# Two attentions on one core: score 0 ahead of the split maximum, and two kinds of copies moved between ScalarE and VectorE

## The chip, the core and the metric

The kernel runs on one core of one Trainium2 chip. The core has a matrix engine (TensorE, PE in the profile, with its weight loads listed apart as PEld), VectorE (DVE), ScalarE (ACT), GpSimd (POOL), and SyncE (SP), which issues most DMAs. Each engine works off its own queue in order; they meet through semaphores. Matmul results land in PSUM, which has eight banks of 128 × 512 f32; this kernel uses seven as a pool (bank0 to bank6) and keeps the eighth (`po`) for the value products. The metric is device time in microseconds, one launch; smaller is better.

## What is computed

Two independent multi-head attentions over 2048 positions, 576 features and 32 heads of 18, with their outputs side by side. Cut to what matters:

```python
# A: each position attends to itself and 7 earlier ones, 2 apart
idx = pos[:, None] - 2 * jnp.arange(8)[None, :]
logits = einsum("bhsd,bhswd->bhsw", q, kg) * scale       # masked where idx < 0
o_a = einsum("bhsw,bhswd->bhsd", softmax(logits), vg)
# B: full attention, 2048 x 2048 per head
p = softmax(einsum("bhqd,bhkd->bhqk", q, k) * scale)
o_b = einsum("bhqk,bhkd->bhqd", p, v)
out = concatenate([o_a @ wo_a, o_b @ wo_b], axis=-1)     # q, k, v = x @ wqkv for each
```

## The kernel before

**Stages.** First come the projections of both parts (L353, L290), mixed with the first maxima. Then a loop over 512 steps does the full attention of part B. Part A's windowed attention runs beside it on GpSimd, with little pieces on the other engines. The output products of both parts are slipped in between.

**The loop over steps.** The heads stand in eight groups `g` of four, the queries in four blocks `b` of 512, the keys in sixteen tiles `kt` of 128; a step is one `(g, b, kt)`, and a block is 16 steps. For each of the four heads of a step, `score` (L256) lets TensorE multiply 128 keys by 512 queries into a bank of the ring "scores" (banks 0 to 3), and ScalarE takes the exponential into a tile `e` (L268). `weigh` (L728), one step later, multiplies `e` by the values into `po` (L731), which adds up over the block's 16 key tiles. The values carry a column of ones, so `po` holds the denominators too.

**Maxima.** The exponential needs each query's maximum over all keys subtracted. The kernel finds it a good way ahead: the scores are computed a second time, transposed, with queries on the partitions (L160), and VectorE reduces a bank to maxima (L168). Once a block has all of them, they are negated, transposed, split and loaded by small DMAs into the spare rows 54 and 55 of the query tile `qs` (`place`, L191), so that the score matmul of 56 rows subtracts them itself. These banks come from the ring "else" (banks 4 to 6). All in all 2048 pieces of 512 keys are reduced.

**Rows of the array.** A head's 54 rows (18 features, three times, as split numbers) lie in the partitions 0 to 63 or 64 to 127, so two matmuls of different halves run at once. Score order in a step is h = 0, 2, 1, 3: 0 and 2 lie in the lower rows, 1 and 3 in the upper.

**Split maxima.** A step gives VectorE three reductions: two of whole pieces (`maximum`, L218, one from each half) and one of a bank that is filled by two half pieces of 256 keys (`parts_of_maximum`, L233), the first from the upper rows and the second from the lower. [...] So the second half waits for a no-op in ScalarE's queue (L243), and that no-op waits for the first half. The no-op is issued before the step's first exponential.

**Order in a step** (L1140 to L1180), as TensorE's queue has it: first half, score 0, whole maximum (upper), score 2, score 1, second half, [an output product, if one is due, "inside" the step], score 3, whole maximum (lower), then the value products of the step before. VectorE gets the reductions in the order whole, split, whole.

**Output products.** A product of part A (`sums_of_a`, L946) or B (`sum_of`, L1044) multiplies by `wo` in two row halves into two banks, `one` and `two` (`beside`, L1022). For A ScalarE copies one sum and VectorE adds the other. For B VectorE copies `one` (L1055) and adds `two` (L1056). Those of B run "inside" a step with `kind` "scores" while more than four pieces of maxima are left, and otherwise stand in `waiting` with no kind; `waiting` is worked off after the scores of a step or at its end. When the maxima have run out, two steps share one run of value products (`paired`), which here is called the tail.

**End of a block.** `finish` (L736) copies `po` into the tile `o` with ScalarE (L740, 31 times; the last block goes through `closing`). A DMA, a reciprocal and GpSimd's multiplication then divide by the denominators, many steps later (L763 to L770). The first value product of the next block waits for this copy, since it overwrites `po`. `producing` is the set of steps in which, by the plan, an output product stands: part A's at `A_FROM + GAP * j + ends[h] + 1` (L973), and B's near the end (L1128). `total` is the number of maxima pieces, `given` counts those already issued.

## Time and profile before

| | |
|---|---|
| Median of 3 runs | 1619.34 us (1617.29 to 1619.95) |
| The profiled execution: its own time | 1616.82 us |
| Its span, first to last instruction | 1615.0 us |
| Mean granted TensorE clock | 0.997 |
| Busy in the stretch 560 to 580 us (of 20.00) | PE 20.00, VectorE 18.68, ScalarE 20.00, GpSimd 19.21 |
| Busy in the stretch 1560 to 1600 us (of 40.00) | PE 40.00, VectorE 10.32, ScalarE 21.63, GpSimd 0.00 |

The page is of one execution; times in it are in us from the span's start. Matmuls overlap at their ends, and so do the instructions of ScalarE and VectorE, so a pace is read from start to start. A bracket at the end of a timeline row gives the idle time before it and what ended that, inferred from semaphores. PE and its weight loads are listed as two engines: PEld can be idle while PE is busy.

### The profile page before, as it was taken

How to read it: one execution, taken by the hardware profiler on the slowest of the kernel's cores; microseconds unless marked ns; L12 is line 12 of the kernel's file. 1: busy time of each engine (PE TensorE's matmuls, PEld its weight loads, DVE VectorE, ACT ScalarE, POOL GpSimd, SP SyncE). 2: the span in 40 equal slices, each digit the busy share in tenths (PEclk: the TensorE clock that was granted, in tenths of full speed). 3: DMA queues.
4: the chain of work that ended last, by engine and by line, in shares of the span. 5: the costliest groups of instructions: out<-in, count | busy, mean ns of one | idle time of the engine just before them, and what ended most of it. 6: DMA issues, size and time to landing. Idle time of an engine off the chain costs nothing.

```text
span 1615.0 us, 35230 instructions
## 1 busy us (share of the span) xinstructions
PE 1599.0 (99%) x13394; PEld 959.5 (59%) x13394; DVE 1393.9 (86%) x2366; ACT 1212.4 (75%) x2419; POOL 961.1 (60%) x792
## 2 busy tenths in 40 slices
PE   9999999999999999999999999999999999999998
PEld 7999888999544444444444444444444444445676
DVE  5199999999899998999999999999999999999532
ACT  6424442121799998999999999999999999998444
POOL 2405742210265995996995995995996997920000
PEclk9999999999999999999999999999999999999999
DMA  8937954432222262254235235332532241034201
GB/s 250 239 121 196 275 164 133 134 104 79 60 56 64 73 147 54 62 118 113 62 85 133 72 98 115 98 91 60 125 106 58 59 135 47 22 124 139 89 38 60
DMA packets 186058, 172.11 MB, mean 107 GB/s; under 512 B 119152, under 2 KB 132976, under 8 KB 184160
## 3 DMA queue, kind: packets, MB, share of 16 engines
q1 hardware_dynamic: 181024, 158.31, 35.3%
q0 software_dynamic: 4032, 10.63, 3.1%
q8 instruction: 105, 1.72, 0.5%
q10 hardware_dynamic: 832, 0.92, 0.2%
q14 instruction: 65, 0.53, 0.1%
HBM read 96.94 MB, written 71.90 MB: 105 GB/s over the span
## 4 chain that ended last, share of the span: by engine, by line
PE 82%; POOL 7%; DVE 5%; DMA 3%; ACT 2%; issue 1%; SPq 0%; POOLq 0%; DVEq 0%; ACTq 0%
PE po L731 24%; PE bank L160 15%; PE bank L353 15%; PE bank L263 15%; PE bank L1036 8%; PE bank L290 5%; DVE mx L168 4%; ACT e L268 2%; POOL pr L868 1%; POOL pr L872 1%; POOL pr L911 1%; DMA akv<-da 1%; DMA dqk<-olo 1%; POOL pr L912 1%; POOL pr L913 0%
## 5 line engine op out<-in xcount | busy, mean ns | idle before, releaser
L168 DVE TENSOR_REDUCE mx<-bank 128x2 f32<-128x512 f32 x2048 | 1286.0, 684 | 114.5 <-PE bank L160 86.2
L268 ACT ACTIVATE e<-bank 128x512 f32<-128x512 f32 x2048 | 1050.2, 607 | 90.3 <-PE bank L263 83.2
L160 PE MATMUL bank<-ks,qs 54*128 54x256 f32 (+1 forms) x2536 | 791.8, 377 | 7.4 <-DVE mx L168 5.9
L160 PEld LDWEIGHTS bank<-ks,qs 54*128 54x128 f32 x2536 | 411.3, 184 | 464.6 <-DVE mx L168 423.4
L263 PE MATMUL bank<-qs,ks 56*128 56x512 f32 x2048 | 567.3, 426 | 0.1
L731 PE MATMUL po<-e,v 128*19 128x512 f32 x4096 | 537.9, 599 | 0.0
L263 PEld LDWEIGHTS bank<-qs,ks 56*128 56x128 f32 x2048 | 299.3, 185 | 14.7 <-issue 7.5
L868 POOL TENSOR_TENSOR pr<-aq,akv 128x1024 f32<-128x1024 f32 x72 | 158.5, 2202 | 15.4 <-DMA akv<-da 12.8
L911 POOL TENSOR_TENSOR pr<-lg,akv 128x1024 f32<-128x1024 f32 x72 | 158.5, 2201 | 0.6
L872 POOL TENSOR_TENSOR pr<-pr 128x1024 f32<-128x1024 f32 x64 | 152.6, 2384 | 5.0
L731 PEld LDWEIGHTS po<-e,v 128*19 128x19 f32 x4096 | 70.5, 97 | 129.4 <-issue 127.0
L681 ACT ACTIVATE ohi<-bank 128x512 f32<-128x512 f32 (+1 forms) x56 | 30.4, 595 | 152.5 <-issue 100.7
L353 PE MATMUL bank<-xhi,ahi 64*128 64x512 f32 (+1 forms) x448 | 113.5, 387 | 0.0
L353 PE MATMUL bank<-xhi,alo 64*128 64x512 f32 (+1 forms) x448 | 112.3, 387 | 0.0
L353 PE MATMUL bank<-xlo,ahi 64*128 64x512 f32 (+1 forms) x448 | 111.9, 388 | 0.1
L912 POOL TENSOR_TENSOR pr<-pr 128x512 f32<-128x512 f32 x72 | 92.5, 1285 | 5.6
L401 POOL TENSOR_TENSOR alo<-raw,ahi 128x512 fp32r<-128x512 f32 (+1 forms) x14 | 17.6, 1258 | 120.7 <-ACT ahi L400 88.8
L493 POOL TENSOR_TENSOR olo<-olo,ohi 128x512 fp32r<-128x512 f32 x36 | 46.2, 1294 | 66.1 <-ACT ohi L492 57.5
L767 POOL TENSOR_TENSOR o<-o,rec 128x512 f32<-128x512 f32 x29 | 37.6, 1297 | 58.7 <-ACT e L268 34.2
L103 POOL CAST mh<-mt 128x32 fp32r<-128x32 f32 x32 | 6.9, 217 | 102.3 <-DVE mt L183 99.5
L353 PEld LDWEIGHTS bank<-xhi,ahi 64*128 64x128 f32 (+1 forms) x448 | 65.0, 181 | 2.9
L353 PEld LDWEIGHTS bank<-xhi,alo 64*128 64x128 f32 (+1 forms) x448 | 63.9, 182 | 2.9
(197 smaller groups left out, 1827.6 us busy)
## 6 DMA issues: line engine op xcount, KB each, us to landing
do<-n SPq DMA_DIRECT2D x28, 512.0 KB
da<-ohi SPq DMA_DIRECT2D x52, 256.0 KB
akv<-da SPq DMA_DIRECT2D x64, 175.5 KB
out<-y SPq DMA_DIRECT2D x32, 288.0 KB
qs<-dqk SPq DMA_DIRECT2D x30, 288.0 KB
ks<-dqk SPq DMA_DIRECT2D x30, 288.0 KB
at<-dao SPq DMA_DIRECT2D x64, 128.0 KB
rec<-drec SPq DMA_DIRECT2D x29, 256.0 KB
```

Of the source, the lines that this page charges most:

```text
L160: return nc.tensor.matmul(ps if part is None else ps[:, 256 * r : 256 * r + 256], qs[at, b, p, 128 * t : 128 * t + 128], ks[at, p, 512 * k ...
L168: nc.vector.tensor_reduce(at, ps.rearrange("q (s n) -> q s n", s=2), axis=AX.X, op=ALU.max)
L263: nc.tensor.matmul(ps, ks[at, p, 128 * kt : 128 * kt + 128], qs[at, b, p], start=True, stop=True)
L268: nc.scalar.activation(e, ps, AF.Exp, scale=SCALE)
L290: nc.tensor.matmul(ps, a, b, start=c == i == 0, stop=c == 4 and i == 1)
L353: nc.tensor.matmul(ps, a, b, start=start, stop=stop)
L731: nc.tensor.matmul(po[32 * i : 32 * i + 19], vs[g][:, kt, 19 * i : 19 * i + 19], es[i], start=kt == 0, stop=kt == NT - 1)
L868: nc.gpsimd.tensor_mul(pr, ap(st["q"][:, 2 * c], (SUB, 2), (0, W), (1, SUB)), window(st["k"], c))
L872: nc.gpsimd.tensor_add(st["pr"], st["pr"], pr)
L911: nc.gpsimd.tensor_mul(at, ap(st["lg"], (0, 2), (SUB, W), (1, SUB)), window(st["v"], c))
L912: nc.gpsimd.tensor_add(at[:, :, :4], at[:, :, :4], at[:, :, 4:])
L1036: nc.tensor.matmul(ps, a, b, start=start, stop=stop)
```

## The change

Four edits, printed with their core:

```diff
-    def score(g, b, kt, h, kind="scores"):
+    def score(g, b, kt, h, kind="scores", between=None):
...
         nc.tensor.matmul(ps, ks[at, p, 128 * kt : 128 * kt + 128], qs[at, b, p], start=True, stop=True)
+        if between:
+            between()
...
-        nc.scalar.activation(o, po, AF.Copy)
+        if step + 1 in producing or sum(given) == total:
+            nc.scalar.activation(o, po, AF.Copy)
+        else:
+
+            nc.vector.tensor_copy(o, po)
+            copied.add(step + 1)
...
     producing = set()
+    copied = set()
...
         one, two = beside(kind, *both)
-        nc.vector.tensor_copy(y, one)
+        if kind:
+            nc.vector.tensor_copy(y, one)
+        else:
+            nc.scalar.activation(y, one, AF.Copy)
         nc.vector.tensor_add(y, two, y)
...
-        parts = bool(begun) or total - sum(given) > 3
+        parts = (bool(begun) or total - sum(given) > 3) and step not in copied
 
         ps = bank() if inside and whole else None
-        if parts:
-            part = parts_of_maximum()
+        part = []
         for h in (0, 2, 1, 3):
 
             if inside and h == 3:
                 inside.pop(0)()
-            es[h] = score(g, b, kt, h)
+
+            es[h] = score(g, b, kt, h, between=(lambda: part.append(parts_of_maximum())) if parts and h == 0 else None)
             if h == 0 and whole:
                 maximum(1, ps)()
             if h == 1 and parts:
-                part()
+                part[0]()
```

In each step with a split maximum, score 0's matmul is issued to TensorE ahead of the first half; the no-op on ScalarE still stands ahead of the first exponential. At the end of a block, where no output product is planned for the next step and maxima are left, VectorE copies `po` in ScalarE's place, and the next step goes without its split maximum, whose two halves are made later. In products of B without a kind, ScalarE copies `one`, and VectorE still adds `two`.

In the built programs, six of the 31 block copies go to VectorE, and 27 of the 30 copies of half a product's sums to ScalarE. The six steps without a split maximum move twelve half pieces on; at the end of the maxima two products of B, which stood in `waiting`, now run inside steps. The number of reductions, 2048, and all other instructions stay.

## The prediction

> **What bounds the kernel now.** I read the page's busy line first, then its chain of waits, then two stretches of the busy-time windows. The columns of a window row are its bounds and length, then the busy time (and count of instructions) of TensorE, its weight loads, VectorE, ScalarE and GpSimd, then granted clock, DMA share and GB/s.

> ```profile
> PE 1599.0 (99%) x13394; PEld 959.5 (59%) x13394; DVE 1393.9 (86%) x2366; ACT 1212.4 (75%) x2419; POOL 961.1 (60%) x792
> PE 82%; POOL 7%; DVE 5%; DMA 3%; ACT 2%; issue 1%; SPq 0%; POOLq 0%; DVEq 0%; ACTq 0%
> ...
> 560.00:580.00 20.00, 20.00 (x160) 8.55 (x154) 18.68 (x32) 20.00 (x40) 19.21 (x18) 1.00 0.50 119
> 1560.00:1600.00 40.00, 40.00 (x470) 29.63 (x466) 10.32 (x23) 21.63 (x43) 0.00 (x0) 1.00 0.10 38
> ```

> In the long stage (the row at 560) TensorE and ScalarE never rest and VectorE hardly does; in the tail (the row at 1560) only TensorE is full. So the question is what sets the pace of one step of the long stage. The timeline of one step answers it; its columns are start, length, engine, line and operation, and the count.

> ```profile
> 558.80 0.38 PE L160 MATMUL bank<-ks,qs 54*128 54x256 f32 x1
> 558.81 0.49 PE L263 MATMUL bank<-qs,ks 56*128 56x512 f32 x1
> 559.03 0.40 PE L160 MATMUL bank<-ks,qs 54*128 54x512 f32 x1
> 559.14 0.52 PE L263 MATMUL bank<-qs,ks 56*128 56x512 f32 x2
> 559.38 0.30 PE L160 MATMUL bank<-ks,qs 54*128 54x256 f32 x1
> 559.51 0.44 PE L263 MATMUL bank<-qs,ks 56*128 56x512 f32 x1
> 559.51 0.43 PE L160 MATMUL bank<-ks,qs 54*128 54x512 f32 x1
> 559.87 1.05 PE L731 MATMUL po<-e,v 128*19 128x512 f32 x8
> 560.86 0.38 PE L160 MATMUL bank<-ks,qs 54*128 54x256 f32 x1
> ...
> 558.80 0.18 PEld L160 LDWEIGHTS bank<-ks,qs 54*128 54x128 f32 x1 [0.85 <-DVE mx L168]
> ...
> 559.29 0.18 PEld L160 LDWEIGHTS bank<-ks,qs 54*128 54x128 f32 x1
> ...
> 561.34 0.18 PEld L160 LDWEIGHTS bank<-ks,qs 54*128 54x128 f32 x1
> 561.43 0.29 PE L160 MATMUL bank<-ks,qs 54*128 54x256 f32 x1
> ...
> 561.56 0.40 PE L160 MATMUL bank<-ks,qs 54*128 54x512 f32 x1
> 561.89 0.14 PEld L731 LDWEIGHTS po<-e,v 128*19 128x19 f32 x8 [0.25 <-issue]
> ...
> 581.21 0.38 PE L160 MATMUL bank<-ks,qs 54*128 54x256 f32 x1
> ...
> 1556.45 1.91 PE L731 MATMUL po<-e,v 128*19 128x512 f32 x16
> 1558.30 0.73 PE L263 MATMUL bank<-qs,ks 56*128 56x512 f32 x4
> ```

> From 558.80 to 581.21 lie 11 steps, so a plain step takes 2.037 us. The "0.85 <-DVE mx" before its first weight load looks like a wait for VectorE, but TensorE is busy with the value products (L731) in that time: the next matmul follows them 0.99 us after they begin (559.87 to 560.86). In the tail, where nothing of VectorE is awaited, sixteen of them take 1.85 us (1556.45 to 1558.30), so eight cost 0.86 and the rest, 0.99, is what eight alone take before anything can follow. The pace is therefore TensorE's own: about 1.05 us from the first half maximum to the first value product, then 0.99.

> What fills the 1.05 us is the handshake of the split maximum. The second half (559.38, rows 0 to 63) may not start before the first half (558.80) is done, and ScalarE's no-op carries that message. The first half ends at 559.18, and the second half's weight load starts 0.11 us later, at 559.29; one step on, 561.24 and 561.34. After it come the second half, the whole maximum 0.13 later, the products 0.33 to 0.36 later. Nothing waits there but for that message.

> **The change, part by part.**

> *Score first.* Score 0 and the first half run on different halves of the array and start within 0.01 us of each other, so swapping them alone moves nothing. But the no-op does not wait for one matmul. In the built program every matmul that signals raises one counter of TensorE, in order, and the no-op waits for a value of it. Before, that value is reached with the first half; in the new order score 0 is counted ahead of it, so the no-op waits for both. The rows above give the two ends: the half of 256 columns ends at 559.18, the score of 512 at 559.30. The message thus leaves 0.12 us later, less the 0.01 by which score 0 starts earlier: 0.11.

> [...]

> How much of 0.11 reaches the step? Take the faster step, from 560.86: weight load at +0.48, second half +0.57, whole maximum +0.70, products +1.03, next step +1.03+0.99 = 2.02. Adding 0.11 to each gives 2.13, against the mean of 2.037: 0.09. The slower step (558.80: load +0.49, second half +0.58, whole maximum +0.71, products +1.07) has 0.04 of other delay in it, which hides behind the new one. Lower bound: zero, if the second half's place were set by its row group, which ends score 2 about then. Upper bound: 0.115 with ScalarE's first exponential, queued behind the no-op, later too. I take 0.08, near the upper end, because the load follows the message in both steps at the same distance.

> How many steps pay is in the rows grouped by line (count, then busy time and mean ns; the first row is count, then shortest, median and longest ns).

> ```profile
> L243 ACTq EVENT_SEMAPHORE  x488: 17/17/17, 418.8 to 1504.8; - x163
> ...
> L168 DVE TENSOR_REDUCE mx<-bank 128x2 f32<-128x512 f32 x2048 | 1286.0, 684 | 114.5 <-PE bank L160 86.2 <-PE bank L353 0.5
> ...
> L740 ACT ACTIVATE o<-po 128x512 f32<-128x512 f32 x31 | 19.5, 628 | 2.5 <-issue 2.5
> ...
> L954 ACT ACTIVATE y<-bank 128x288 f32<-128x288 f32 x32 | 13.2, 412 | 18.2 <-PE bank L1036 17.4 <-issue 0.9
> ...
> L1055 DVE COPY y<-bank 128x288 f32<-128x288 f32 x24 | 10.9, 456 | 49.0 <-PE bank L1036 49.0
> ```

> Of 488 handshakes 32 stand in steps with a product of part A and 62 in the two steps beside each of the 31 copies: 394 plain steps at 0.08 are 31.5 us. The 32 product steps are full on TensorE as well, at 0.10: 3.2. In the 62 the exponentials, late by the copy, cover most of it: I take 0.03, 1.9 (none to 0.11 are the bounds). Cost so far 36.6 us.

> The score first also gains. At the first step of a block, score 0 waits for its block's negated maxima from many DMA queues; before, these waits are worked off only after the first half is issued.

> ```profile
> 482.73 0.38 PE L160 MATMUL bank<-ks,qs 54*128 54x256 f32 x1
> 483.08 0.18 PEld L263 LDWEIGHTS bank<-qs,ks 56*128 56x128 f32 x1 [0.17 <-issue]
> 483.11 0.47 PE L263 MATMUL bank<-qs,ks 56*128 56x512 f32 x1
> ...
> 483.62 2.07 ACT L268 ACTIVATE e<-bank 128x512 f32<-128x512 f32 x4 [0.33 <-PE bank L160]
> ...
> 485.09 0.38 PE L160 MATMUL bank<-ks,qs 54*128 54x256 f32 x1
> ...
> 485.55 0.63 ACT L740 ACTIVATE o<-po 128x512 f32<-128x512 f32 x1
> ...
> 487.21 0.38 PE L160 MATMUL bank<-ks,qs 54*128 54x256 f32 x1
> ...
> 489.60 0.38 PE L160 MATMUL bank<-ks,qs 54*128 54x256 f32 x1
> ```

> Score 0 comes 0.38 us after the half instead of 0.01, and the step takes 2.36 instead of 2.04. With the score first these waits lie under the value products of the step before: 0.32 saved, at the 11 blocks whose first score has this long list of queues in the built program: 3.5 us.

> *VectorE copies the sums.* The condition leaves it to six of the 31 copies: the blocks that end at steps 16, 32, 48, 64, 80 and 464. There ScalarE's 0.63 us copy pushes the exponentials; the two steps after it take 2.12 and 2.39, together 0.43 too long, six times 2.6. No row shows VectorE copying 512 columns. It lies between the 288-column copy (0.456) and twice that (0.91); I take 0.69, like the reduction of the same width. It stands behind a reduction, the next block's value products wait for it, and it ends about 0.1 later than ScalarE's copy: 0.6 back. Left out in those six steps are two half maxima each, with one reduction and its handshake; they return at the end, as more maxima beside two products that before ran alone: 6 reductions with some 0.12 us of TensorE each, 0.7 (zero if covered, 6 × 0.684 = 4.1 if VectorE sets that stretch). Net gain 1.3 us.

> *ScalarE copies in the tail.* 27 of the 30 copies of half a product's sums move. The row of L954 shows ScalarE doing the same shape in 0.412 against 0.456. TensorE waits for this copy where only four scores lie between two products:

> ```profile
> 1553.75 0.46 DVE L1055 COPY y<-bank 128x288 f32<-128x288 f32 x1 [1.67 <-PE bank L1036]
> ...
> 1553.97 2.07 ACT L268 ACTIVATE e<-bank 128x512 f32<-128x512 f32 x4 [0.55 <-PE bank L263]
> ...
> 1554.26 0.18 PEld L1036 LDWEIGHTS bank<-qs,qs 62*128 62x128 f32 x1 [0.30 <-DVE y L1055]
> ```

> Queued behind the copy on ScalarE are the next four exponentials (1553.97), 0.22 after the copy begins; they may slip by 0.2 and their reader, the value products at 1556.45, has 0.4 to spare. So 0.05 at some 18 places: 0.8 gained (0 to 1.2). Were that cover gone, 18 times 0.2, 3.6, would be lost.

> *Sum.* 36.6 − 3.5 − 1.3 − 0.8 = +31 us on the profiled execution's own 1616.8, so 1647.8. It was 2.5 below the median of the runs shown, 1619.34; against that median I predict 1650.

> **The rivals.**

> *The handshake costs nothing* (the other side: faster). If the second half's place in its row group, not the message, sets its start, everything else of the sum remains: −5.6, so 1614. For it: score 2 (559.14, 512 columns) holds that row group until about 559.4 at the 0.13 that 256 columns hold it (559.38 to 559.51), and the half starts at 559.38, a tie. Against it: its weight load starts only with the message, 0.11 after the half's end. It decides if the load-to-matmul time can shrink by 0.11; it is 0.09.

> *Half of it is covered.* At 0.04 a plain step: 394 × 0.04 + 1.6 (products) + 1.0 (copies) − 5.6 = +13, 1632.

> *All of it and the exponentials too.* The first exponential stands behind the no-op; if it sets the next step's scores, 0.115 in every step: 488 × 0.115 − 5.6 = +50, 1670. Against it: four exponentials take 2.07 (the row at 483.62), less than the longer step.

> *The score hides VectorE's waits.* If the 0.85 before each step were true idle time, a score in front would save its own 0.22 (558.81 to 559.03) in 488 steps, 107 us: 1512. The tail's 1.85 against 0.99 speaks against it.

> **How the numbers follow.** My forecast (0.06 to 0.10 a step) has 0.70, from 1642 to 1658 around 1650; half covered 0.08, all of it 0.10, no cost 0.11, the hidden waits 0.01. The range 1632 to 1665 leaves out the faster rivals and the far end of the dearest. A measurement of this kernel can tell about 0.2%, 3.2 us, from no change: faster 0.12, within 0.02 (the half-covered case with less still), slower 0.86.

> **What would show it.** Right: in a plain step score 0 first, then the half; the second half's weight load at +0.60 instead of +0.49; the step at 2.11 to 2.13, with no more alternation of 2.02 and 2.06; ScalarE's share of the long stage falling below 20.00 in 20. The first steps of the 11 blocks lose their 0.32. Wrong: the load at +0.49 and a step of 2.04, or VectorE's copy ending so late that the two steps after it stay at 4.5. The forecast also fails if the end of a half behind a longer score could count alone.

## The result, and the profile after

| | before | after |
|---|---|---|
| Median | 1618.32 us (4 runs, 1615.92 to 1619.95) | 1654.48 us (4 runs, 1654.35 to 1657.48) |
| Profiled execution: its own time, its span | 1616.82, 1615.0 | 1654.35, 1652.6 |
| Mean granted clock | 0.997 | 1.0 |

The changed kernel is slower: a ratio of 1.0231, 95% interval 1.0214 to 1.0247. The two profiled executions lie 37.5 us apart where the sum of the prediction was 31; the median is 4.5 us above the forecast of 1650, inside the range from 1632 to 1665.

The busy line and the chain that ended last of the changed kernel:

```profile
PE 1643.9 (99%) x13390; PEld 946.4 (57%) x13390; DVE 1386.8 (84%) x2345; ACT 1230.9 (74%) x2440; POOL 960.4 (58%) x792
PE 97%; DVE 1%; POOL 1%; DMA 0%; issue 0%; ACT 0%; POOLq 0%; DVEq 0%
```

Two stretches of its busy-time windows, columns as before:

```profile
560.00:580.00 20.00, 20.00 (x152) 7.97 (x148) 17.82 (x31) 19.05 (x38) 18.99 (x20) 1.00 0.51 112
1560.00:1600.00 40.00, 40.00 (x473) 29.77 (x468) 8.13 (x20) 24.64 (x53) 2.68 (x6) 1.00 0.08 32
```

In the long stage ScalarE has fallen from 20.00 to 19.05 and VectorE from 18.68 to 17.82; TensorE stays full. The chain went from 82% to 97% TensorE: no other engine sets the pace anywhere for long. TensorE's busy time grew by 45 us, but its matmuls did not become more. Rows of matmuls overlap, so a wait can lie under the row in front of it: in the step below, the row of the two scores at 501.84 lasts until 502.35, past the load at 502.13 that had to wait. Such a wait shows as busy time, not as idle time.

One step of the changed kernel in its timeline, TensorE and its weight loads:

```profile
501.50 0.49 PE L263 MATMUL bank<-qs,ks 56*128 56x512 f32 x1
501.50 0.18 PEld L160 LDWEIGHTS bank<-ks,qs 54*128 54x128 f32 x1
501.50 0.61 PE L160 MATMUL bank<-ks,qs 54*128 54x256 f32 x2
501.84 0.51 PE L263 MATMUL bank<-qs,ks 56*128 56x512 f32 x2
502.13 0.18 PEld L160 LDWEIGHTS bank<-ks,qs 54*128 54x128 f32 x1 [0.21 <-ACTq L243]
502.13 0.38 PE L160 MATMUL bank<-ks,qs 54*128 54x256 f32 x1
502.35 0.39 PE L160 MATMUL bank<-ks,qs 54*128 54x512 f32 x1
502.67 1.05 PE L733 MATMUL po<-e,v 128*19 128x512 f32 x8
503.65 0.49 PE L263 MATMUL bank<-qs,ks 56*128 56x512 f32 x1
```

(L263 is the score, L733 the value products, L743 and L746 the block copies, L1064 and L1066 the copies of half a product.) Score 0 is issued first, then the first half and the whole maximum of the upper rows. The second half's weight load stands at 502.13, 0.63 behind the first matmul; before it was 0.48 and 0.49. From there on everything follows at its old distance: the value products 0.54 behind the load (0.55 and 0.58 in the two steps shown of before), the next step 0.98 behind the products. The step takes 2.15.

What the waits and the groups of instructions say of the changed kernel (waits: us in total, times, longest; groups: busy time, mean ns, idle time ahead):

```profile
PEld bank L263 <- ACT e L270: 415.9, 494, 0.8
...
PEld bank L160 <- ACTq L243: 101.1, 467, 0.3
```

```profile
L743 ACT ACTIVATE o<-po 128x512 f32<-128x512 f32 x25 | 15.8, 630 | 1.7 <-PE po L733 1.7
...
L1066 ACT ACTIVATE y<-bank 128x288 f32<-128x288 f32 x21 | 8.6, 412 | 8.6 <-PE bank L1044 8.0
...
L746 DVE COPY o<-po 128x512 f32<-128x512 f32 x6 | 4.1, 681 | 0.0
```

The row with 494 waits is the apparent wait of the prediction: 0.84 each, while the value products run. It only changed its name, from VectorE's `mx` to ScalarE's `e`, since another matmul now stands first. The row behind it is new and real: 467 loads of a second half wait for ScalarE's no-op, 0.22 each.

**Where the 37.5 us went.** A step is taken here from the first matmul behind one run of value products to the first behind the next. Steps are numbered from the first one so taken, so a number given for a step of a trace is two below the program's `step`.

| steps | count | mean before | mean after | sum |
|---|---|---|---|---|
| plain (2.00 to 2.10 before) | 389 | 2.033 | 2.162 | +50.3 |
| with an output product | 31 | 4.162 | 4.269 | +3.3 |
| first of the 11 blocks | 11 | 2.317 | 2.156 | −1.8 |
| the two behind VectorE's six copies | 12 | 2.260 | 2.094 | −2.0 |
| others over 2.10 before | 37 | 2.325 | 2.193 | −4.9 |
| the two at 619 to 631 us | 2 | 5.987 | 3.222 | −5.5 |
| tail, from step 482 | 18 | | | −0.7 |
| ahead of the loop | | | | −1.2 |

So plain steps lost more than was forecast, and more than half of the surplus came back in places that the prediction had not counted. The largest single one is a stall of the kernel before:

```profile
621.31 1.26 POOL L875 TENSOR_TENSOR lg<-pr 128x512 f32<-128x512 f32 x1
622.61 0.43 DVE L886 TENSOR_TENSOR am<-lg 128x256 f32<-128x256 f32 x1 [3.38 <-POOL lg L875]
...
623.68 0.58 PE L160 MATMUL bank<-ks,qs 54*128 54x256 f32 x1 [2.85 <-DVE mx L168]
```

```profile
620.00:640.00 20.00, 17.14 (x125) 9.08 (x117) 14.34 (x27) 13.23 (x27) 6.93 (x6) 0.83 0.33 81
```

VectorE's first maximum of part A (L886) stands in its queue ahead of reductions, and GpSimd had not finished the logits (L875). VectorE waited 3.38 us, TensorE ran out of free banks and idled 2.85, and its granted clock was 0.5 for 6.8 us, from 0.4 before the matmuls went on (0.83 on the mean of these 20 us). The changed kernel comes to this step about 6 us later, GpSimd is in time, and the clock stays at 1.00 until 1650.9 us, 3.7 us behind the last matmul.

### The profile page after: what moved, and what is told of

It reads as the page before. It is cut to its first block, busy times and chain, and to the rows that moved or that the text cites. A ratio compares the mean times of both kernels' runs of the same rounds, so it can differ in the third digit from the quotient of the medians.

```text
span 1652.6 us, 35222 instructions
## 1 busy us (share of the span) xinstructions
PE 1643.9 (99%) x13390; PEld 946.4 (57%) x13390; DVE 1386.8 (84%) x2345; ACT 1230.9 (74%) x2440; POOL 960.4 (58%) x792
## 4 chain that ended last, share of the span: by engine, by line
PE 97%; DVE 1%; POOL 1%; DMA 0%; issue 0%; ACT 0%; POOLq 0%; DVEq 0%
PE po L733 30%; PE bank L263 21%; PE bank L160 19%; PE bank L355 15%; PE bank L1044 7%; PE bank L292 5%; POOL xlo L403 1%; DVE mx L168 0%; PE bank L507 0%; DMA more<-xa 0%; DMA out<-y 0%; PE bank L1019 0%; ACT vs L573 0%; POOL xhl L438 0%; DVE am L894 0%
## 5 line engine op out<-in xcount | busy, mean ns | idle before, releaser
L168 DVE TENSOR_REDUCE mx<-bank 128x2 f32<-128x512 f32 x2048 | 1288.1, 684 | 154.9 <-PE bank L160 142.2
L270 ACT ACTIVATE e<-bank 128x512 f32<-128x512 f32 x2048 | 1061.7, 606 | 89.7 <-PE bank L160 35.0
L160 PE MATMUL bank<-ks,qs 54*128 54x256 f32 (+1 forms) x2532 | 836.9, 390 | 1.3 <-DVE mx L168 0.9
L263 PE MATMUL bank<-qs,ks 56*128 56x512 f32 x2048 | 578.6, 429 | 0.0
L263 PEld LDWEIGHTS bank<-qs,ks 56*128 56x128 f32 x2048 | 303.1, 184 | 424.0 <-ACT e L270 415.9
L733 PE MATMUL po<-e,v 128*19 128x512 f32 x4096 | 537.6, 599 | 0.0
L160 PEld LDWEIGHTS bank<-ks,qs 54*128 54x128 f32 x2532 | 398.2, 184 | 110.9 <-ACTq L243 101.1
L733 PEld LDWEIGHTS po<-e,v 128*19 128x19 f32 x4096 | 70.5, 97 | 130.1 <-issue 125.2
L774 POOL TENSOR_TENSOR o<-o,rec 128x512 f32<-128x512 f32 x29 | 37.5, 1292 | 62.0 <-DMA rec<-drec 39.6
L103 POOL CAST mh<-mt 128x32 fp32r<-128x32 f32 x32 | 6.9, 215 | 110.8 <-DVE mt L183 110.8
```

Of the source, the lines that this page charges most:

```text
L160: return nc.tensor.matmul(ps if part is None else ps[:, 256 * r : 256 * r + 256], qs[at, b, p, 128 * t : 128 * t + 128], ks[at, p, 512 * k ...
L168: nc.vector.tensor_reduce(at, ps.rearrange("q (s n) -> q s n", s=2), axis=AX.X, op=ALU.max)
L263: nc.tensor.matmul(ps, ks[at, p, 128 * kt : 128 * kt + 128], qs[at, b, p], start=True, stop=True)
L270: nc.scalar.activation(e, ps, AF.Exp, scale=SCALE)
L733: nc.tensor.matmul(po[32 * i : 32 * i + 19], vs[g][:, kt, 19 * i : 19 * i + 19], es[i], start=kt == 0, stop=kt == NT - 1)
```

## The experiments

All times are medians; the kernel before, run beside them, had 1616.34 (first four), 1616.64 (next four) and 1616.67 (last four).

**1. The first edit alone, and the change without it.**

score_first_only is the kernel before with `between` in `score` and its call, as in the diff of the change; undo_score_first is the changed kernel with this:

```diff
-        part = []
+        part = [parts_of_maximum()] if parts else []
...
-            es[h] = score(g, b, kt, h, between=(lambda: part.append(parts_of_maximum())) if parts and h == 0 else None)
+            es[h] = score(g, b, kt, h)
```

> The kernel before with score 0 in front of the first half and no other edit. Late message: 1654 to 1660 us, the plain step at 2.16, the second half's weight load at +0.63, slightly slower than the changed kernel, since the gains of the copies are missing. If the copies have a part in the loss: below 1645.

> The changed kernel with the first half in front of score 0 again; both kinds of moved copies are kept. If the late message (the no-op that now also waits for score 0) makes the whole loss: 1613 to 1618 us, a little below the kernel before, the plain step back at 2.04 with its alternation of 2.02 and 2.06, the second half's weight load at +0.49. If the moved copies have a part in the loss: above 1625.

Measured: score_first_only 1657.29 (1656.06 to 1657.65), ratio 1.025 (1.0235 to 1.0266), median step 2.158. undo_score_first 1623.81 (1622.06 to 1626.35), ratio 1.005 (1.0033 to 1.0067), median step 2.033. So the first edit alone makes the whole loss, and a little more than the whole change has. The step of the undo came out as expected; its total did not, it missed by 6 us. Experiment 5 takes that up.

**2. The message without the order.** The order of the kernel before, but the no-op waits for score 0 as well as for the first half. TensorE's queue is untouched, and the no-op still stands ahead of the first exponential. The core of it:

```diff
+        def message(scored):
+            said.append(nc.scalar.nop())
+            sync(said[0], one)
+            sync(said[0], scored)
...
+        mine = nc.tensor.matmul(ps, ks[at, p, 128 * kt : 128 * kt + 128], qs[at, b, p], start=True, stop=True)
+        if between:
+            between(mine)
```

> The kernel before, in its own order on TensorE, but the no-op waits for score 0 beside the first half. Late message: the loss without any change of order; score 0 is done at about +0.51, so the message about 0.11 later than before, second half's load at +0.60, step 2.12 to 2.13, 1645 to 1655 us; nearly all of the loss. If the place of score 0 in TensorE's queue were the cause (weights loaded in another order, the half a place later): 1618, step 2.04.

Measured: 1649.48 (1648.11 to 1650.53), ratio 1.0203 (1.0188 to 1.0218). Two steps of its timeline:

```profile
499.90 0.38 PE L160 MATMUL bank<-ks,qs 54*128 54x256 f32 x1
499.90 0.18 PEld L267 LDWEIGHTS bank<-qs,ks 56*128 56x128 f32 x1
499.90 0.50 PE L267 MATMUL bank<-qs,ks 56*128 56x512 f32 x1
...
500.50 0.18 PEld L160 LDWEIGHTS bank<-ks,qs 54*128 54x128 f32 x1 [0.19 <-ACTq L246]
...
502.02 0.38 PE L160 MATMUL bank<-ks,qs 54*128 54x256 f32 x1
...
502.62 0.18 PEld L160 LDWEIGHTS bank<-ks,qs 54*128 54x128 f32 x1 [0.18 <-ACTq L246]
```

The load stands at +0.60, where the prediction had put it, and the 389 plain steps have a mean of 2.130. Nothing but the message was made later, and 0.097 of the 0.129 a step is there. The other 0.032 comes with the order: the step's load is then at +0.63. The traces also hold the times at which TensorE's counter, for whose values the no-op waits, goes up. Medians of the 389 steps, in us behind the step's first matmul:

| | before | wait_both | half_score_first | after |
|---|---|---|---|---|
| counter goes up for the first half | 0.397 | 0.397 | 0.431 | 0.544 |
| counter goes up for score 0 | 0.513 | 0.514 | 0.397 | 0.510 |
| no-op | 0.418 | 0.535 | 0.453 | 0.565 |
| second half's weight load | 0.484 | 0.600 | 0.518 | 0.631 |

(half_score_first is experiment 3; its score 0 is the first 256 columns.) In all four the no-op follows the last rise of the counter that it waits for by 0.021 to 0.022, and the load follows the no-op by 0.065 to 0.066. In the changed kernel the counter goes up for the half 0.034 behind score 0, though the half has half the columns and was issued 0.004 behind. No two rises of this counter lie closer than 0.034 in any trace here, and those of score and half, of equal length in half_score_first, lie as far apart. So the other 0.03 is the distance of two rises of the counter.

**3. A shorter score ahead.** The changed kernel, with score 0's matmul in two of 256 columns, and only the first of them ahead of the first half. The core of it:

```diff
         if between:
+            nc.tensor.matmul(ps[:, :256], ks[at, p, 128 * kt : 128 * kt + 128], qs[at, b, p, :256], start=True, stop=True)
             between()
+            nc.tensor.matmul(ps[:, 256:], ks[at, p, 128 * kt : 128 * kt + 128], qs[at, b, p, 256:], start=True, stop=True)
```

> The changed kernel, but only the first 256 of score 0's 512 columns stand in front of the first half, the other 256 behind it as a matmul of their own. Late message: the no-op now waits for a score of 256 columns, which ends 0.11 earlier than one of 512; second half's load at +0.51 to +0.54, step 2.04 to 2.08, 1618 to 1635 us with the extra weight load. If any score in front, whatever its length, is what costs: 1650 or more.

Measured: 1630.83 (1630.21 to 1632.54), ratio 1.009 (1.0075 to 1.0105), median step 2.065 (before 2.029); its total holds a stall as in experiment 5. One step of its timeline:

```profile
500.33 0.38 PE L264 MATMUL bank<-qs,ks 56*128 56x256 f32 x1
...
500.34 0.38 PE L160 MATMUL bank<-ks,qs 54*128 54x256 f32 x1
...
500.85 0.18 PEld L160 LDWEIGHTS bank<-ks,qs 54*128 54x128 f32 x1
```

The load is back at +0.52. With a score in front that is as long as the half, the message is 0.03 later than before, by the distance of two rises alone, and so is the step (0.036). The rest of the price, 0.10 a step, follows the length of what is counted ahead, not the fact of an order.

**4. No message in the path.** The changed kernel, but the second half stands behind score 3 and the lower whole maximum ahead of it, so the message has time to spare.

```diff
+        plain = parts and whole and not inside
...
-            if h == 1 and parts:
+            if h == (1 if plain else 3) and whole:
+                maximum(0)()
+            if h == (3 if plain else 1) and parts:
                 part[0]()
-            if h == 3 and whole:
-                maximum(0)()
+        if plain:
+            rings["else"].append(rings["else"].pop(0))
```

> The changed kernel with the second half moved behind score 3, the lower whole maximum ahead of score 3 in its place, and the ring of three banks turned by one each plain step; product steps keep their order. Late message: it arrives long before the second half is due, so the loss is gone though score 0 is still in front: 1610 to 1622 us, step 2.01 to 2.05. If score 0 in front costs by itself, or if VectorE gets its banks too late in this order: 1640 or more, with first weight loads that wait for VectorE.

Measured: 1635.11 (1632.8 to 1635.47), ratio 1.0109 (1.0095 to 1.0122), between the two. Steps alternate between two lengths (from its timeline: first matmuls, the lower whole maxima and the loads of score 3):

```profile
499.26 0.49 PE L263 MATMUL bank<-qs,ks 56*128 56x512 f32 x1
...
499.85 0.49 PE L160 MATMUL bank<-ks,qs 54*128 54x512 f32 x1
500.03 0.18 PEld L263 LDWEIGHTS bank<-qs,ks 56*128 56x128 f32 x1
...
501.45 0.50 PE L263 MATMUL bank<-qs,ks 56*128 56x512 f32 x1
...
502.02 0.40 PE L160 MATMUL bank<-ks,qs 54*128 54x512 f32 x1
502.03 0.18 PEld L263 LDWEIGHTS bank<-qs,ks 56*128 56x128 f32 x1
...
503.45 0.49 PE L263 MATMUL bank<-qs,ks 56*128 56x512 f32 x1
```

Only 32 loads still wait for the no-op, as many as there are steps with a product, and one plain step in two (501.45 to 503.45) takes 2.00, as short as the shortest of before (2.005): in these steps score 0 in front costs nothing by itself. The other (2.19) is new. In it score 3's load stands at +0.77 instead of +0.58, and in 170 of the 181 such steps it follows a rise of ScalarE's counter by less than 0.06 (median 0.043). By the ring of the banks it waits for the last exponential of the step before. The exponentials stand behind the no-op in ScalarE's queue, and the no-op is as late as in the changed kernel (0.565 instead of 0.418). That this lateness makes every other step long is likely, but was not tested. So the experiment shows that the message's way to the second half can be made free; it does not show that the whole loss goes with it.

**5. The other two edits alone.** block_copies_only is the kernel before with VectorE's block copies, and with their steps without a split maximum; tail_copies_only is the kernel before with ScalarE's copies of half a product's sums.

> The kernel before with VectorE's six block copies alone. By the prediction 1.3 us gained; by the changed kernel's trace, where the step after the copy has 2.03 and the next nothing to catch up, up to 2.5: 1615.5 to 1617.5. If the maxima that are moved to the end cost more than they save: 1619 to 1621.

> The kernel before with ScalarE's copies in the tail alone. By the prediction 0.8 us gained: 1617 to 1618, within what can be told from no change; the tail's steps 0.04 to 0.10 shorter. If the exponentials behind the copies are late for the value products: 1619 to 1622.

Measured: tail_copies_only 1616.65 (1614.07 to 1618.17), ratio 0.9994 (0.9982 to 1.0006); the stretch from step 489 on took 94.8 us against 95.5, the forecast 0.8 and less than can be told in the total. block_copies_only 1625.71 (1623.53 to 1628.69), ratio 1.0052 (1.0038 to 1.0067): the edit loses 8 to 9 us where 1.3 were to be gained. The six copies did gain: 2.13 and 2.39 became 2.10 and 2.02. The loss stands in three steps, which took 9.59, 3.63 and 2.88 instead of 2.61, 2.10 and 2.01. Its timeline, read backwards, gives the way there (SPq rows are DMA issues):

```profile
987.40 0.20 POOL L103 CAST mh<-mt 128x32 fp32r<-128x32 f32 x1
...
1022.77 0.58 SPq L770 DMA_DIRECT2D rec<-drec  x1
...
1035.55 1.28 POOL L771 TENSOR_TENSOR o<-o,rec 128x512 f32<-128x512 f32 x1 [9.11 <-DMA rec<-drec]
...
1110.33 1.26 POOL L880 TENSOR_TENSOR lg<-pr 128x512 f32<-128x512 f32 x1
...
1111.62 1.47 DVE L891 TENSOR_TENSOR am<-lg 128x256 f32<-128x256 f32 x1 [6.34 <-POOL lg L880]
...
1114.34 0.58 PE L160 MATMUL bank<-ks,qs 54*128 54x256 f32 x1 [7.47 <-DVE mx L168]
```

The same places in the kernel before:

```profile
976.58 0.23 POOL L103 CAST mh<-mt 128x32 fp32r<-128x32 f32 x1
...
1011.58 0.59 SPq L766 DMA_DIRECT2D rec<-drec  x1
...
1024.19 1.29 POOL L767 TENSOR_TENSOR o<-o,rec 128x512 f32<-128x512 f32 x1
...
1098.92 1.29 POOL L875 TENSOR_TENSOR lg<-pr 128x512 f32<-128x512 f32 x1
```

The steps without a split maximum move pieces on, so from step 64 on every block has its maxima one to three steps later. GpSimd's cast of them (L103) then falls behind other work of its queue, here by 10.8 us (the loop had begun 2.7 us later in this execution); the small DMAs that load the maxima wait for it in SyncE's queue, and all that SyncE issues behind them is 11 us later, the block's reciprocals (`rec`) too. GpSimd waits 9.11 us for these, finishes part A's logits 11.4 us later, and VectorE and TensorE stand still as at 621 us. The windows show the clock:

```profile
1100.00:1120.00 20.00, 12.53 (x84) 5.62 (x80) 11.87 (x22) 10.62 (x22) 16.14 (x12) 0.74 0.12 35
```

The undo has the same three long steps (8.05, 3.64 and 2.84), hence its missing 6 us. The changed kernel does not have them, although its maxima come as many steps later: its slower loop seems to give GpSimd the time. Only the last links of this chain were put to the test, in experiment 7; its head is read from the rows.

**6. Score first only where it gains.** The changed kernel, with the new order in the 11 steps that begin a block alone.

```diff
+        ahead = step in (16, 32, 48, 64, 80, 384, 400, 432, 448, 464, 480)
+        part = [parts_of_maximum()] if parts and not ahead else []
```

> The changed kernel with score 0 in front only in the 11 first steps of a block whose score waits for all the DMA queues; the first half in front in all other steps. Late message and the block starts as the prediction has them (2.36 down to 2.16 in these 11 steps): 2 to 3 us below the run with the first half always in front, 1611 to 1615, the fastest of all. If the waits for the queues cost the same wherever they stand: no difference from the run with the first half always in front.

Measured: 1624.58 (1622.13 to 1625.61), ratio 1.0045 (1.0032 to 1.0057), no better than the undo's 1623.81. The 11 steps did fall, to 2.16 or 2.17, but the step at 1104 took 9.66 in place of the undo's 8.05.

**7. Part A's maxima two steps later.** All pieces of part A from its first maximum on are due two steps later, so that GpSimd has 4 us more: in the kernel before (later_a_alone), in block_copies_only (later_a_copies), in the undo (later_a_undo) and in score_first_at_blocks (later_a_at_blocks).

```diff
-        pieces = [(33, lower), (35, exponents), (39, share), (60, upper), (61, rest), (64, lambda: put(0)), (66, lambda: put(1))]
+        pieces = [(35, lower), (37, exponents), (41, share), (62, upper), (63, rest), (66, lambda: put(0)), (68, lambda: put(1))]
...
-        pieces[:0] = [(at, lambda f=f, n=n: f(n)) for f, ats in ((most, (31, 32, 33)), (total, (36, 37, 38)),
+        pieces[:0] = [(at, lambda f=f, n=n: f(n)) for f, ats in ((most, (33, 34, 35)), (total, (38, 39, 40)),
...
```

> The kernel before, with part A's maxima and all that comes behind them due two steps later; no edit of the change. Theory (VectorE's first maximum of part A waits for GpSimd's last product in front of it, TensorE runs dry behind it for 2.85 us and its clock is then halved for some us): the stall at 621 us goes, steps 94 and 95 come down from 4.94 and 7.03 us together to about 4.2, no row with a granted clock of 0.5 is left: 1608 to 1612. Rival (the stall at 621 us has another cause, or moves on with the pieces): 1615 to 1618.

> VectorE copies the blocks' sums where no product follows, as in the change, and part A's maxima and what follows are due two steps later. Theory: both stalls (at 621 and at 1110 us) go, the gain of the six copies is left: 1605 to 1611 against 1625.7 for the copies without the later pieces. Rival (the copies on VectorE cost by themselves): 1618 to 1626.

> The change without its first edit (first part of the maxima ahead of the first scores again), part A's pieces two steps later. Theory: 1604 to 1610 against 1623.8 without the later pieces, which shows what the second and third edits are worth where GpSimd is in time. Rival (the two edits lose by themselves): 1618 to 1625.

> First scores ahead of the first part of the maxima only in the 11 steps that begin a block without products, second and third edits kept, part A's pieces two steps later. Theory: the 11 steps lose about 0.3 us each against the same kernel without them, no stall: 1601 to 1607. Rival (the first scores' waits are hidden by nothing there): the same as the kernel without them, within 1 us.

| kernel | without | two steps later | ratio to before |
|---|---|---|---|
| before | 1616.67 | 1613.76 | 0.9984 (0.9975 to 0.9993) |
| block_copies_only | 1625.71 | 1617.58 | 1.0002 (0.9992 to 1.0012) |
| undo_score_first | 1623.81 | 1615.89 | 0.9998 (0.9987 to 1.0009) |
| score_first_at_blocks | 1624.58 | 1614.61 | 0.9988 (0.9979 to 0.9996) |

The three with VectorE's copies came down by 8 to 10 us, the kernel before by 3. In the latter the stall is gone: VectorE waits 0.38 instead of 3.38, and the clock of that stretch is 1.00.

```profile
624.68 0.42 DVE L886 TENSOR_TENSOR am<-lg 128x256 f32<-128x256 f32 x1 [0.38 <-POOL lg L875]
```

```profile
610.00:640.00 30.00, 29.12 (x240) 13.22 (x240) 28.09 (x48) 27.74 (x56) 18.74 (x13) 1.00 0.29 73
```

Steps 94 and 95, 11.97 us together, became 6.20, as expected; but later steps gave 3.5 us of it back, where the moved pieces now fall. With the copies GpSimd is still late around 1100, less so. From the timeline and the windows of later_a_copies:

```profile
1106.55 0.48 PE L160 MATMUL bank<-ks,qs 54*128 54x256 f32 x1 [3.79 <-DVE mx L168]
```

```profile
1100.00:1120.00 20.00, 16.21 (x116) 6.53 (x112) 15.34 (x27) 14.65 (x30) 8.59 (x8) 0.91 0.29 73
```

So all four missed their expected totals by 2 to 8 us, though each in the expected direction. It shows that GpSimd's lateness, not the copies, made most of their loss: of 9 us against the kernel before, 4 are left against later_a_alone (1617.58 and 1613.76), and the trace of later_a_copies still has the wait of 3.79 us shown above. That the copies gain anything in the total was not shown. The first scores at the 11 blocks: 1614.61 against 1615.89, close to the expected rival's 1 us, though in the traces the 11 steps fell by about 0.2 each.

The best of these, later_a_alone, is 0.16% below the kernel before. That is under what the prediction took as the bound of the measurement.

## Why the prediction was right, point by point

- **What bounds the kernel: right.** TensorE's own sequence with the handshake in it. Making nothing but the message later made the kernel 2.0% slower (experiment 2). That the two halves of a bank need such a message was not shown: all kernels here have it.
- **The no-op waits for score 0 too: right, the term mis-sized.** Forecast 0.11 later and 0.08 a step; measured 0.147 later (0.631 against 0.484) and 0.129. The smaller part is the share that reaches the step: the prediction's own working gave 0.09, it took 0.08, and experiment 2 gives 0.097 of 0.116. The slower of the two alternating steps hides some 0.04, as the prediction had it: those under 2.033 before grew by 0.148, the others by 0.107. Since 0.148 is all of the message's lateness, nothing is left for a second cause. The larger part was missing: the counter goes up for the half not with score 0 but 0.034 behind it, in the step at 501.50 at 502.009 for score 0 and at 502.043 for the half. In the changed kernel the counter does not go up for the half at 0.397, as it does where the half stands first, but at 0.544, behind the score. When the half itself ended, the counter does not tell. With the 0.034 the upper bound of 0.115 a step would not have stood.
- **Product steps, 3.2: right** (31 single ones, 3.3).
- **Steps beside the copies, 1.9 lost: miscounted.** The prediction took these 62 steps, the product steps and the plain ones as three separate kinds. In the trace 24 of the 62 are product steps themselves. Another 24 follow one, were not late (2.013), and paid the full price (2.160). Two lie in the tail. Only the 12 beside the six copies that move were late, and they became 2.0 us shorter together.
- **Other late steps: no term.** 37 more steps over 2.10 became 4.9 us shorter together (2.325 to 2.193). The longer message seems to cover part of what had made them late, a late exponential or a late bank; this was not followed up.
- **First steps of 11 blocks, 0.32 gained: right.** In nine of them 2.33 to 2.37 became 2.15 to 2.17. That is the 0.32 less the 0.13 that these steps pay like all others, as the sum had counted it; two of the 11 (2.14 and 2.20 before) had had little of it.
- **VectorE's copies, 1.3 gained: the price right (0.681 for 0.69), the conclusion wrong for the edit by itself.** The step that failed is "they return at the end": the pieces moved on also make the maxima of the blocks between later, and through three queues (read from the rows, tested in part) that cost 8 to 9 us. The changed kernel does not have these long steps, which is why its total didn't show it.
- **ScalarE's copies in the tail, 0.8: right** (0.7 in the tail).
- **The stall at 619 to 631 us: not seen.** The trace of before has a step of 7.03 us there and a clock of 0.83; the prediction read the stretch at 560 and took it for the whole loop. It gave 5.5 us back. With the 4.9 of the other late steps it hid that the dear term was 19 us too small: without these two the median would stand near 1665, at the edge of the range. That it came out 4.5 us from the forecast is in part luck.
- **The rivals.** "No cost" fell with the load at +0.63 and, without a new order, with experiment 2. "Half covered" fell with the mean of 2.162. "All of it and the exponentials" comes near in size (0.129 for 0.115 a step), but by another way: the faster steps grew by no more than the message (0.148 for 0.147), ScalarE has free time now, 19.05 of 20, and the surplus comes with the order on TensorE (experiment 2 against score_first_only, 2.130 against 2.160). "The hidden waits" fell with the result: the 0.85 ahead of each step stayed (0.84).

## What to carry to other kernels

The no-op that waits on TensorE's counter came 0.021 to 0.022 us behind the last rise up to its value, whichever matmul raised it, so a score counted ahead of the half made the message 0.147 later: before an instruction is put in front of another, ask which message it thereby delays and what stands behind that message. A loop that is slowed or sped by a few us meets its side engines in another phase: here VectorE's waits for GpSimd, 3.38 us in the kernel before and 6.34 in block_copies_only, went with 2.85 and 7.47 us of idle time on TensorE, and an expected gain of 1.3 us turned into a loss of 8 to 9. Before a total is trusted, the gains and losses should be summed by kinds of steps: here a term that was 19 us too small and 10 us of gains that no term had counted made it look better than it was.
